# A decode step of attention plus MLP on one core: longer loops on VectorE and TensorE, side work moved to GpSimd and ScalarE, another form for the last P V

## The chip, the cores and the metric

One Trainium2 chip, of which the kernel uses one core. The metric is the device time of one execution in microseconds, the median of several runs. The profile is one more execution, recorded by the hardware profiler; its span runs from the first to the last recorded instruction, and its own device time is 1.84 us longer than that span.

## The reference

The sizes are B = 8 sequences of one token, D = 576, H = 32 heads of 128, a cache of 4096 positions, and an MLP of width 4608. All inputs are bf16.

```python
g = sigmoid((x * gate_w).sum(-1, keepdims=True))
q = (x @ wq) as [B, 32, 1, 128]
p = softmax(einsum("bhqd,bhkd->bhqk", q, k_cache) * 128 ** -0.5)
a = einsum("bhqk,bhkd->bhqd", p, v_cache) as [B, 1, 4096] @ wo
h = gelu(layernorm(x) @ w1 + b1)            # tanh form
b = h @ w2 + b2
out = g * a + (1 - g) * b
```

The two caches are 268 MB each, so nearly all of the 557 MB that the kernel reads is K and V, each byte used once.

## The kernel before, in words

**Groups.** The work is cut into 32 groups (`NG`), each of one sequence and eight heads. A group's K is 8.4 MB. It is laid out with 16 partitions per head and 256 positions per partition, and comes as two halves into the buffers KB[0] and KB[1]. Its V has the same layout and comes as one 8.4 MB transfer into VB. All large transfers stand in one hand-written order on SyncE's queue: K halves of group n+1, then V of group n+1, and so on. Each waits for the release of its buffer: a K half for the multiplication that read it last, V for the last P V matmul of the group before.

**Scores.** Eight chunks of 32 positions per group. `mult` has VectorE multiply K by the broadcast query (4096 products per partition, result in `p1`); TensorE adds up the products in eight matmuls with the identity (`held` keeps the weights in place for seven of them); `reduce` has VectorE add the last 16 partial sums. `between(c)` is the place where other work goes between the chunks: `norm` of the group before, the MLP's up projection, its down projection, and the output projection `a_proj`.

**Softmax and P V.** `softmax` finds maxima on VectorE, has ScalarE do the exponential, and has VectorE spread the weights into P with eight masked multiplications (`own`). `pv` has 64 matmuls, 32 columns of P as weights and 512 columns of V moving, into four row groups of one PSUM bank. `evict` (ScalarE) copies the bank to `O_sb`, `gather` adds the four row groups up with four fp32 matmuls, `norm` divides, `put` stores.

**The last group's V** comes in eight parts, because the end of the kernel hangs on it: half of it into KB[0], and 32, 32, 16, 16, 16, 8 and 8 positions into VB (`V_LAST`). All of its P V is in another form, `pv_turned`: one matmul per position, with V as the weights and eight columns of P moving, so that no `evict` and `gather` stand behind the last transfer.

**The MLP** shares one buffer, RB, with all weights in turn: wq, w1, w2, wo. `up_proj` (216 matmuls) stands in groups 1 to 3, `act_h` (bias and gelu, five operations on VectorE and a sigmoid on ScalarE) in group 4, `down_proj` (144 matmuls) in group 5; wo is loaded after it. `b_out` adds b2 and multiplies by 1 - g.

**The program.** A small recording layer (`Stream`) keeps one list of operations per engine and one semaphore per engine. Groups 6 to 29 (`L0`, `L1`) are emitted as a hardware loop on VectorE and TensorE (`emit_loop`), in which a wait's value grows by a fixed step with each turn; everything else is emitted in full. `head_slot` sets at which slot of a 256-slot code block the loop's first instruction stands. ScalarE, SyncE and GpSimd have no loop.

Counted in the built program, with a matmul as its weight load and its multiplication (twice that for fp32, one for a `held` one):

| instructions | TensorE | VectorE |
|---|---|---|
| ahead of the loop | about 2,185 | 241 |
| in the loop's body | 234 | 57 |
| behind the loop | about 1,075 | 71 |

## Time and profile before

| | |
|---|---|
| three runs | 1304.11, 1305.06, 1305.33 us, median 1305.06 |
| profiled execution | 1304.64 us, span 1302.8 us |
| busy: PE, DVE, ACT, POOL | 812.6, 855.5, 65.1, 1.6 us |
| mean TensorE clock granted | 0.84 |
| mean rate of HBM reads | 428 GB/s over the span |
| multiplication by q on DVE (L430), x256 | 2282 ns each |
| chunk sum on DVE (L448), x256 | 684 ns each |
| one matmul of a usual P V (L491), x1984 | 534 ns mean |

PE, PEld, DVE, ACT, POOL and SP are TensorE's multiplications, its weight loads, VectorE, ScalarE, GpSimd and SyncE. The profile has a row per DMA queue: q1 is SyncE's, q10 ScalarE's, and q8 and q14 carry the engines' own code. A share of 1.00 of the DMA engines means that all 16 are busy all the time. In a list of instructions, the first two numbers are the start and the time taken (a merged entry: of the whole run of them), and the bracket tells how long the engine was idle before and what released it. In a list of stretches, each row gives per engine the busy time and (x the number of instructions), and at its end TensorE's clock, the DMA engines' share and GB/s.

### The profile page before, as it was taken

The numbers are of one execution on the slowest core, as the hardware profiler recorded it, in microseconds if no ns is written. First come the engines' busy times: TensorE is split into PE (matmuls) and PEld (weight loads), VectorE is DVE, ScalarE is ACT, GpSimd is POOL, SyncE is SP. The second block draws the span as 40 slices with busy tenths as digits, with TensorE's granted clock in tenths as the row PEclk, the third lists the DMA queues.
The fourth block names the chain that finished last, engine by engine and source line by source line (L and its number), as shares of the span: only waits on it lengthen the run. The fifth ranks groups of instructions, "written<-read, shape, count | busy, mean of one in ns | idle before, by whom it ended". The sixth has DMA issues, their size and how long they took to land.

```text
span 1302.8 us, 10855 instructions
## 1 busy us (share of the span) xinstructions
PE 812.6 (62%) x5156; PEld 171.6 (13%) x3364; DVE 855.5 (66%) x1094; ACT 65.1 (5%) x144; POOL 1.6 (0%) x12
## 2 busy tenths in 40 slices
PE   3657776566466565665665666565666656666666
PEld 0112230111011100111110111110011110011113
DVE  4656668456666677666668666668766667766685
ACT  1100001000000000000000000000000000000000
POOL 0000000000000000000000000000000000000000
PEclk8968888678788889878888878888987898887888
DMA  9999999999999999999999999999999999999997
GB/s 401 417 451 425 440 419 427 441 431 410 442 431 431 424 433 434 443 435 433 424 433 431 440 433 435 432 428 432 433 440 429 434 428 433 434 442 429 423 432 304
DMA packets 20900, 557.25 MB, mean 428 GB/s; under 512 B 2048, under 2 KB 6160, under 8 KB 7056
## 3 DMA queue, kind: packets, MB, share of 16 engines
q1 hardware_dynamic: 20624, 556.95, 99.4%
q8 instruction: 13, 0.21, 0.1%
q10 hardware_dynamic: 256, 0.03, 0.0%
q14 instruction: 7, 0.06, 0.0%
HBM read 556.96 MB, written 0.01 MB: 428 GB/s over the span
## 4 chain that ended last, share of the span: by engine, by line
DMA 69%; DVE 18%; PE 9%; issue 3%; SPq 0%; DVEq 0%; ACT 0%
DMA KB<-in_A_k_cache_dram 67%; DVE p L430 16%; PE psb L174 7%; DVE s_sb L448 2%; DMA VB<-in_A_v_cache_dram 2%; PE psb L441 1%; SPq L257 0%; PE psb L491 0%; DVEq L132 0%; PE psb L553 0%; DVE P L477 0%; PE psb L498 0%; ACT E L474 0%; DVE mA L465 0%; PE psb L589 0%
## 5 line engine op out<-in xcount | busy, mean ns | idle before, releaser
L430 DVE TENSOR_TENSOR p<-KB,q_n 128x4096 bf16<-128x4096 bf16 x256 | 581.5, 2282 | 322.7 <-DMA KB<-in_A_k_cache_dram 313.6
L174 PE MATMUL psb<-p,ident 128*128 128x512 bf16 x1792 | 486.1, 417 | 0.0
L441 PE MATMUL psb<-p,ident 128*128 128x512 bf16 x256 | 111.1, 434 | 295.9 <-DVE p L430 295.8
L448 DVE TENSOR_REDUCE s_sb<-psb 128x32 f32<-128x512 f32 x256 | 175.2, 684 | 81.9 <-PE psb L174 81.6
L491 PE MATMUL psb<-VB,P 128*32 128x512 bf16 x1984 | 176.7, 534 | 0.0
L441 PEld LDWEIGHTS psb<-p,ident 128*128 128x128 bf16 x256 | 26.1, 102 | 718.7 <-DVE p L430 637.1
L498 PE MATMUL psb<-rs,ones 128*128 128x8 f32 x64 | 18.8, 368 | 150.9 <-DVE rs L481 150.4
L491 PEld LDWEIGHTS psb<-VB,P 128*32 128x32 bf16 x1984 | 64.3, 129 | 98.6 <-issue 83.4
L477 DVE TENSOR_SCALAR P<-E,own 128x256 bf16<-128x256 bf16 x248 | 51.4, 282 | 17.9 <-ACT E L474 17.9
L508 PE MATMUL psb<-selO,O_sb 128*128 128x8 f32 x248 | 33.6, 262 | 21.2 <-ACT O_sb L503 21.2
L498 PEld LDWEIGHTS psb<-rs,ones 128*128 128x128 f32 x64 | 15.8, 306 | 201.8 <-DVE rs L481 201.3
L418 ACT ACTIVATE q_n<-q_bc 128x128 bf16<-128x128 bf16 x32 | 9.9, 309 | 528.8 <-DVE p L430 528.8
L508 PEld LDWEIGHTS psb<-selO,O_sb 128*128 128x128 f32 x248 | 30.8, 195 | 36.1 <-ACT O_sb L503 36.1
L503 ACT ACTIVATE O_sb<-psb 128x512 f32<-128x512 f32 x31 | 18.5, 596 | 258.7 <-PE psb L491 258.7
L474 ACT ACTIVATE E<-s_sb,mD 128x256 bf16<-128x256 f32 x32 | 16.2, 507 | 143.2 <-DVE mD L473 143.2
L528 PEld LDWEIGHTS psb<-yT_sb,RB 128*128 128x128 bf16 (+1 forms) x216 | 19.4, 165 | 22.0 <-issue 20.0
L423 ACT ACTIVATE OT_sb<-O_n 128x8 bf16<-128x8 bf16 x31 | 7.4, 237 | 252.2 <-DVE O_n L514 252.2
L528 PE MATMUL psb<-yT_sb,RB 128*128 128x8 bf16 (+1 forms) x216 | 19.8, 227 | 0.0
L465 DVE TENSOR_REDUCE mA<-s_sb 128x1 f32<-128x256 f32 x32 | 13.4, 420 | 1.1
L480 DVE TENSOR_REDUCE es<-E 128x1 f32<-128x256 bf16 x32 | 13.2, 411 | 0.0
L513 DVE RECIPROCAL rz<-psb 128x8 f32<-128x8 f32 x31 | 6.2, 200 | 4.7 <-PE psb L508 4.7
L394 PE MATMUL psb<-RB,p 128*8 128x512 bf16 x40 | 5.4, 618 | 5.4 <-DMA RB<-in_A_wq_dram 5.4
(71 smaller groups left out, 100.2 us busy)
## 6 DMA issues: line engine op xcount, KB each, us to landing
KB<-in_A_k_cache_dram SPq DMA_DIRECT2D x64, 4096.0 KB, 26.8
VB<-in_A_v_cache_dram SPq DMA_DIRECT2D x2, 4096.0 KB, 23.8
RB<-in_B_w_dram SPq DMA_DIRECT2D x1, 5184.0 KB, 43.7
RB<-in_B_w_dram SPq DMA_DIRECT2D x1, 4608.0 KB, 45.5
RB<-in_A_wo_dram SPq DMA_DIRECT2D x1, 4608.0 KB, 45.4
RB<-in_A_wq_dram SPq DMA_DIRECT2D x1, 4096.0 KB, 12.6
KB<-in_A_v_cache_dram SPq DMA_DIRECT2D x1, 4096.0 KB, 17.1
VB<-in_A_v_cache_dram SPq DMA_DIRECT2D x2, 1024.0 KB, 20.3
```

The source lines that it names most:

```text
L174: return e.add_instruction(mybir.InstMatmult(name=nc.get_next_instruction_name(), engine=mybir.EngineType.PE, ins=[e.lower_ap(rhs), e.lowe ...
L430: v_mult[n, c] = op("vector", lambda e: e.tensor_tensor(out=p1[:, par, :, :], in0=KB[u % NKH][:, t0:t0 + CT, :], in1=qb, op=ALU.mult), [k_ ...
L441: fn = lambda e, r=r: e.matmul(tr_ps[par][:, :], lhsT=ident[:, :], rhs=r, start=True, stop=False)
L448: v_red[n, c] = op("vector", lambda e: e.tensor_reduce(out=s_sb[:, c * CT:(c + 1) * CT], in_=tr_ps[par][:, :].rearrange("p (t c) -> p t c" ...
L465: t = op("vector", lambda e: e.tensor_reduce(out=mA[:, 0:1], in_=s_sb[:, :], axis=AX.X, op=ALU.max), [v_red[n, NC - 1], c_mA])
L474: a_exp[n] = op("scalar", lambda e: e.activation(out=E[:, :], in_=s_sb[:, :], func=ACT.Exp, bias=mD[:, 0:1], scale=1.0), [v_nm[n], v_P.get ...
L477: v_P[n] = op("vector", lambda e, h=h: e.tensor_scalar(out=(P if n < NG - 1 else P_last)[:, :, h, :], in0=E[:, :].rearrange("p (q t) -> p ...
L491: p_pv[n] = op("tensor", lambda e, o=o, tq=tq, at=at, buf=buf: e.matmul(o, lhsT=P[:, tq, :, :].rearrange("p h t -> p (h t)"), rhs=buf[:, a ...
L498: p_z[n] = op("tensor", lambda e: e.matmul(oz_ps[:, HB:2 * HB], lhsT=ones[:, :], rhs=rs[:, :], start=True, stop=True), [v_rs[n], v_norm.ge ...
L503: a_ev[n] = op("scalar", lambda e: e.activation(out=O_sb[:].rearrange("p t d -> p (t d)"), in_=o_ps[0][:, :], func=ACT.Copy), [p_pv[n], p_ ...
L508: p_oz[n] = op("tensor", lambda e, tt=tt: e.matmul(oz_ps[:, 0:HB], lhsT=O_sb[:, tt, :], rhs=selO[:, tt, :], start=(tt == 0), stop=(tt == T ...
L528: st["p_up"] = op("tensor", lambda e, w=w, o=o, kt=kt: e.matmul(o, lhsT=w, rhs=yT_sb[:, kt, :], start=(kt == 0), stop=(kt >= NKF)), [*ld_w ...
```

## The change

1. **Loops.** VectorE's loop covers groups 1 to 29 and its first instruction stands at slot 128; TensorE's covers groups 4 to 29, at slot 16. For this each engine gets two semaphores: operations of a turn count on the first, those marked `aside` (set-up, MLP, output projection) on the second, so that a turn's counts stay regular. A first turn that lacks some waits is now allowed.
2. **Side work off VectorE.** Clearing PSUM (five banks before, three now), `Sel`, `spread` and the four copies into `g4` go to ScalarE; the gelu chain goes to GpSimd, with a copy out of PSUM by ScalarE ahead of it; `b_out` becomes a copy on ScalarE, and `b_gate`, two operations on GpSimd, takes place in group 27.
3. **The MLP earlier.** `up_proj` in groups 1 and 2, in every chunk; `act_h` and `down_proj` in group 3. w2 and wo are loaded earlier, w2 ahead of the V of group 3. b2 is loaded in group 27, as eight small transfers of five and three rows in place of four of eight rows.
4. **The last P V.** The first 192 of the 256 positions of the last group are done by `pv` with the weights `P_last` into the second bank, followed by `evict` and `gather`; the last 64 stay turned, and both parts are added up in one PSUM region (`qb_ps`). `gather` of group 30 stands ahead of it.

In the built program TensorE now has about 1,745 instructions ahead of its loop and about 800 behind it; VectorE has 53 and 72. ScalarE's list grows from 160 to 181, GpSimd's from 11 to 23, SyncE's stays at 116.

```diff
-        self.sem = {e: nc.alloc_semaphore(f"sem_{e}") for e in ("gpsimd", "scalar", "vector", "tensor")}
+        self.sem = {(e, side): nc.alloc_semaphore(f"sem_{e}{side}")
+                    for e in ("gpsimd", "scalar", "vector", "tensor") for side in range(2)}
...
-        with eng.bass.Fori(0, len(turns), engines=OrderedEngineSet([eng.engine]), head_slot={eng.engine: 0}) as k:
+        with eng.bass.Fori(0, len(turns), engines=OrderedEngineSet([eng.engine]), head_slot={eng.engine: slot}) as k:
...
+    def aside(engine, fn, waits=()):
+        return op(engine, fn, waits, side=1)
...
-    c_ps = [memset("vector", bank[i][:, :], 0.0) for i in range(4)]
-    c_yps = memset("vector", y_ps[:, :], 0.0)
+    def blank(ps):
+        return aside("scalar", lambda e: e.activation(out=ps[:, :], in_=zeros, func=ACT.Copy), [c_mA])
+
+    c_ps = [blank(tr_ps[i]) for i in range(2)]
+    c_yps = blank(y_ps)
...
+    last = NG - 1
+    UP, NUP = 1, 2
+    DN = UP + NUP
+    AP = 30
+    LOOP = {"tensor": DN + 1, "vector": 1}
+    SLOT = {"tensor": 16, "vector": 128}
...
-                o = o_ps[0][32 * j:32 * j + 32, :]
+                o = o_ps[n // last][32 * j:32 * j + 32, :]
...
-                    o, lhsT=P[:, tq, :, :].rearrange("p h t -> p (h t)"),
+                    o, lhsT=(P if n < last else P_last)[:, tq, :, :].rearrange("p h t -> p (h t)"),
...
-        t = op("vector", lambda e: e.tensor_tensor(
-            out=hb.rearrange("p (f b) -> p f b", b=B), in0=up_ps[:, 0:NJ * B].rearrange("p (f b) -> p f b", b=B),
-            in1=b1b, op=ALU.add), [st["p_up"], ld_b1])
+        t = aside("scalar", lambda e: e.activation(out=hb, in_=up_ps[:, 0:NJ * B], func=ACT.Copy), [st["p_up"]])
+        hbv = hb.rearrange("p (f b) -> p f b", b=B)
+        t = op("gpsimd", lambda e: e.tensor_tensor(out=hbv, in0=hbv, in1=b1b, op=ALU.add), [t, ld_b1])
...
-            for i in range(4)]
+            for i in range(4) for r, m in ((0, 5), (5, 3))]
...
-    UP, NUP = 1, 3
-    DN = UP + NUP + 1
-    AP = 30
-    L0, L1 = DN + 1, 30
...
     pv(last - 1, (1,))
     evict(last - 1)
-    pv_turned(last, (0,))
     gather(last - 1)
     norm(last - 1)
+    pv(last, (0,))
     total(last)
     recip(last)
-    pv_turned(last, range(1, 1 + len(V_LAST)))
+    pv(last, (1, 2))
+    evict(last)
+    pv_turned(last, (3,))
+    gather(last)
+    pv_turned(last, range(4, 1 + len(V_LAST)))
     norm_turned(last)
```

## The prediction

> **What bounds the kernel now.** I read the page's DMA rows first, then the same rows for the stretch in which both loops run, then the end of the kernel in quarters of a microsecond.

> ```profile
> span 1302.8 us, 10855 instructions
> DMA packets 20900, 557.25 MB, mean 428 GB/s; under 512 B 2048, under 2 KB 6160, under 8 KB 7056
> q1 hardware_dynamic: 20624, 556.95, 99.4%
> q8 instruction: 13, 0.21, 0.1%
> q14 instruction: 7, 0.06, 0.0%
> ...
> KB<-in_A_k_cache_dram SPq DMA_DIRECT2D x64, 4096.0 KB, 26.8
> ```

> SyncE's queue is busy 99.4% of 16 engines' span, 1295 of 1302.8 us. A K half takes 26.8 us from issue to landing, while its 4.19 MB need 9.8 us at 428 GB/s: some 17 us of earlier transfers are still ahead of it when it is issued. So between the first and the last transfer no engine's work sets the time, as long as this lead isn't used up. What remains is the DMA engines' own order, and the stretch behind the last byte.

> The code transfers are the interesting small rows. By stretch (23 to 76, 76 to 290, 290 to 1230, 1230 to 1290, 1290 to 1298 us), the rows that name code:

> ```profile
> q8 instruction: 1, 0.02, 0.1%
> q14 instruction: 1, 0.01, 0.0%
> ...
> q8 instruction: 8, 0.13, 0.2%
> q14 instruction: 3, 0.02, 0.0%
> ...
> q1 hardware_dynamic: 14446, 406.26, 100.4%
> q14 instruction: 2, 0.02, 0.0%
> ...
> q8 instruction: 2, 0.03, 0.2%
> ...
> q8 instruction: 2, 0.03, 1.7%
> ```

> q8 has nine packets before both loops run, none in 940 us of them and four behind: the pattern of TensorE's code, 2,185 instructions ahead of its loop and 1,075 behind, so one packet per 250 or so. q14's four packets up to 290 us I put down to VectorE (241 instructions and the jump into its loop), the two inside the loops to ScalarE and SyncE, which have none. One packet is short (1.7% of 16 engines in 8 us, over two packets: 1.09 us each), but it stands on one DMA engine, whose share of K and V is late from then on. A transfer is complete only when the latest engine is done. The end of the kernel shows how late:

> ```profile
> 1292.75:1293.00 0.25, 0.00 (x0) 0.00 (x0) 0.21 (x2) 0.00 (x0) 0.00 (x0) 0.50 0.80 311
> 1293.75:1294.00 0.25, 0.25 (x15) 0.25 (x14) 0.17 (x1) 0.00 (x0) 0.00 (x0) 0.50 0.56 221
> 1294.50:1294.75 0.25, 0.25 (x16) 0.25 (x14) 0.00 (x0) 0.00 (x0) 0.00 (x0) 0.50 0.33 131
> 1295.75:1296.00 0.25, 0.25 (x16) 0.25 (x14) 0.00 (x0) 0.00 (x0) 0.00 (x0) 0.50 0.07 25
> 1296.50:1296.75 0.25, 0.25 (x16) 0.25 (x14) 0.00 (x0) 0.00 (x0) 0.00 (x0) 0.50 0.02 8
> 1296.75:1297.00 0.25, 0.24 (x10) 0.15 (x6) 0.00 (x0) 0.00 (x0) 0.00 (x0) 0.50 0.00 0
> 1292.75:1297.00 4.25, 3.79 (x122) 3.70 (x122) 0.57 (x3) 0.24 (x1) 0.00 (x0) 0.50 0.34 131
> ```

> The last three numbers are TensorE's clock, the DMA engines' share and GB/s. One engine alone makes 25. The first engines finish at 1292.75; at 1294.0 about nine run, at 1294.7 five, from 1295.9 one, which ends at about 1296.8. I read steps of 1.5 us: seven engines hardly delayed, four delayed by one q8 packet, four by two, and one, 4.1 us late, by four q14 packets of about 1 us. Thirteen q8 packets over eight engines in turn give just that (the thirteenth comes when its engine is done).

> Behind the last byte:

> ```profile
> 1297.12 0.29 PEld L589 LDWEIGHTS psb<-p,VB 128*128 128x128 bf16 x8 [0.22 <-DMA VB<-in_A_v_cache_dram]
> 1297.88 1.13 PE L553 MATMUL psb<-RB,OT_sb 128*8 128x144 bf16 x32 [0.38 <-DVE OT_sb L598]
> 1299.45 0.66 SPq L257 DMA_DIRECT2D out_dram<-out_sb  x2
> ```

> TensorE waited only 0.22 us for the last eight positions: it was nearly late itself. From 1297.12 to the end at 1302.8 runs a fixed chain of 5.7 us.

> **The change part by part**, against the profiled execution's 1304.64 us.

> *Loops: minus 1.1 us.* TensorE's program shrinks to 1,745 and 800 instructions: seven packets ahead of the loop and three behind, ten for thirteen. In turn over eight engines, two engines get two and six get one. The last of the three is due some 520 instructions behind the loop, which is in the last group's P V, at about 1288 and still ahead of the last V parts. VectorE's 53 instructions end near the loop's head at slot 128, so I count one q14 packet on its engine, one or two microseconds' delay at most. The latest engine is then one with two q8 packets, which now end at about 1295.8, against 1296.8: I take 1.1 us off. Bounds: nothing, if VectorE's engine keeps four packets; and minus 2.7 us, all 16 ending together (the whole stretch from 1292.75 on moves 4.25 us at its rate in the last row, 0.56 MB, which 16 engines at 25 GB/s each move in 1.4 us, so by 1294.15). The packets that fall away free 0.06 MB, which the latest engine doesn't feel.

> [...]

> *The last P V: nothing, if it keeps pace.* These rows price it:

> ```profile
> 1283.02 1.91 PE L491 MATMUL psb<-VB,P 128*32 128x512 bf16 x32
> 1258.53 3.60 PE L491 MATMUL psb<-VB,P 128*32 128x512 bf16 x32
> 1287.58 3.40 PE L589 MATMUL psb<-p,KB 128*128 128x8 bf16 x128 [2.65 <-DVE p L477]
> 1290.84 1.85 PE L508 MATMUL psb<-selO,O_sb 128*128 128x8 f32 x8
> 1285.65 0.58 ACT L503 ACTIVATE O_sb<-psb 128x512 f32<-128x512 f32 x1
> 1228.83 4.49 DVE L430 TENSOR_TENSOR p<-KB,q_n 128x4096 bf16<-128x4096 bf16 x2 [8.73 <-DMA KB<-in_A_k_cache_dram]
> ```

> 192 turned positions at 27 ns (3.40 over 128) go, 5.1 us; 48 usual matmuls come, at 60 ns (1.91 over 32) 2.9 us, or at 113 ns (3.60 over 32, which I take for the half clock that the quarters above grant) 5.4 us, with an evict of 0.58 and a gather of 1.85. Does this end ahead of the last part? The piece that counts starts when position 192 has landed. The last 64 positions are 2.1 MB, a sixteenth of it 131 KB, 5.2 us at 25 GB/s. In these 5.2 us TensorE has to do eight P V matmuls (0.9 at half clock), ScalarE the evict (0.65 with its signal), TensorE the gather (1.85) and 40 turned ones (1.1): 4.5 us. It fits by 0.7 us, so the last eight positions still wait for their transfer. I take 0; bounds plus 0.7 us, if every wait between the engines costs 0.25 us more than in the rows, and minus 0.5, if the last projection (1.13 us at 1297.88) runs at the full clock, where the row of the same 32 matmuls below has 0.67. VectorE, which runs without a pause from the K landing at 1228.83 on, starts up to 2.5 us earlier (the latest engine is 1.6 late there, not 4.1), so P is ready before V.

> *The MLP earlier, on other engines: 0.* It lies in groups whose cover is the 17 us lead.

> ```profile
> 1269.02 0.67 PE L553 MATMUL psb<-RB,OT_sb 128*8 128x144 bf16 x32
> 96.67 1.66 PE L528 MATMUL psb<-yT_sb,RB 128*128 128x8 bf16 x18
> 97.59 0.68 DVE L448 TENSOR_REDUCE s_sb<-psb 128x32 f32<-128x512 f32 x1
> 98.19 2.28 DVE L430 TENSOR_TENSOR p<-KB,q_n 128x4096 bf16<-128x4096 bf16 x1
> 98.48 1.67 PE L174 MATMUL psb<-p,ident 128*128 128x512 bf16 x7
> 205.69 0.46 DVE L539 TENSOR_TENSOR Q<-Q 128x288 f32<-128x288 f32 x1
> ```

> A chunk costs VectorE 2.28 + 0.68, near 3 us, and TensorE 1.67 + 0.39 for the sums plus at most 1.7 for 18 up-projection matmuls, 3.8 us. Eight chunks are 30 us in place of 24, softmax and P V some 9: a group of 39 us, where its 16.8 MB take 39. K's second half is released 6 us later, of 17. w2 now stands ahead of V of group 3 on SyncE and waits for `up_proj`; V would wait for group 2's P V anyway, and w2's 5.3 MB fill the queue for 12 us meanwhile. `down_proj` waits on TensorE for w2, and the sums of chunks 6 and 7 queue behind it for about 6 us; VectorE has by then multiplied chunk 7 and so released K. On GpSimd I price five gelu operations at 0.5 us (0.46 on VectorE) up to 2 us each; ScalarE stands in its sigmoid for up to 8 us, with the next query copy and exponential queued behind it, which are due 10 us and more later. Should the lead fail, the loss would be the 6 us beyond it; I see no way to use it up.

> [...]

> *Set-up: 0.* ScalarE gets 12 operations and one more table load ahead of the query projection.

> ```profile
> 6.42 1.28 ACT L348 ACT_TABLE_LOAD   x1
> 7.72 0.20 ACT L348 ACTIVATE stat<-stat 8x1 f32<-8x1 f32 x1
> 18.64 0.60 ACT L397 ACTIVATE Q<-psb 128x512 bf16<-128x512 f32 x1 [10.72 <-PE psb L394]
> 15.14 5.37 PE L394 MATMUL psb<-RB,p 128*8 128x512 bf16 x40 [5.40 <-DMA RB<-in_A_wq_dram]
> ```

> Three table loads are 3.8 us, four operations of 0.6 and ten of 0.2 are 4.4 us: from 1.8 us on done by about 11, and the projection waits for wq until 15.1. Cover 4 us; without it the first K release would be late, again inside the lead.

> *b2 in eight transfers:* 9 KB in group 27, in the same lead; 0, bounds minus and plus 0.1.

> **Sum:** 1304.64 - 1.1 = 1303.54. The profiled execution lies 0.42 below the median of the runs, so for the median I forecast 1303.9.

> **The rivals.**
> 1. *No gain (1304.4 to 1305.5).* VectorE's jump to slot 128 needs further packets, or the P V chain at the end takes the 1.1 us up (0.7 plus half a microsecond of clock phase). For it: TensorE's wait of only 0.22 us. Against: its 4.5 of 5.2 us.
> 2. *More gain (1302.0 to 1302.5).* The doubled engines don't double, as if the packets ran over all 16: the latest is 1.5 late, 2.6 us off, 3.1 with the last projection at the full clock. For it: only ten packets. Against: the five engines left at 1294.7.
> [...]
> 4. *Slower by a used-up lead (1307 to 1310).* w2 ahead of V starves the queue in group 3 for the 3 to 6 us of the late chunks. Against: 17 us.

> **How the numbers follow.** Forecast 0.64, rivals 0.14, 0.12, 0.03 and 0.04, 0.03 for none of these. What a measurement can tell here is about 0.2%, 2.6 us: under 1302.45 faster, over 1307.67 slower. Faster has most of rival 2 (0.11) and 0.02 of the rest, 0.13. Slower has rivals 3 and 4 and 0.01 of the rest, 0.08. Within the bound lie the other 0.79. The range takes the forecast's bounds from 1302.3 (2.7 off) to 1305.7 (0.7 on), widened for the runs' own spread of 0.6 to 1301.9 and 1306.2.

> **What would show it.** Right: ten q8 packets, three of them behind 1230 us; up to two q14 packets before 60 us and none at the loops' entry; the DMA engines' rate in the last quarters falling to nothing 4.1 - 1.1, about 3 us after the first engine is done, with two engines, not five, in the last microsecond; and TensorE's last eight turned matmuls still released by the VB transfer. Wrong: q8 or q14 packets in every turn; DMA share under 0.9 anywhere between 50 and 1290 us; the last turned matmuls released by `gather`; or a last transfer that ends no earlier.

## The result, and the profile after

The changed kernel takes 1302.97 us (median of 21 runs, 1302.61 to 1304.00), the kernel before 1304.94 us (21 runs, 1304.11 to 1305.66). The ratio is 0.9986, with a 95% interval from 0.9979 to 0.9992: 1.97 us less. That lies inside the range forecast, and 0.93 us under the forecast of 1303.9. The range, 1301.9 to 1306.2, also holds the time of the unchanged kernel, so that the parts of the sum have to be looked at one by one.

First the code packets, from the page of the kernel after, in the columns packets, MB and share:

```profile
span 1301.0 us, 10743 instructions
...
q1 hardware_dynamic: 20624, 556.95, 99.6%
q8 instruction: 10, 0.16, 0.1%
...
q14 instruction: 4, 0.03, 0.0%
```

Ten q8 packets for 13, as counted, and four q14 for 7. Then the end in quarters of a microsecond (the last three numbers again TensorE's clock, the DMA engines' share, GB/s; one DMA engine alone makes 25):

```profile
1294.00:1294.25 0.25, 0.25 (x3) 0.25 (x3) 0.00 (x0) 0.00 (x0) 0.00 (x0) 0.50 0.21 82
...
1295.25:1295.50 0.25, 0.25 (x13) 0.25 (x13) 0.00 (x0) 0.00 (x0) 0.00 (x0) 0.50 0.11 41
1295.75:1296.00 0.25, 0.23 (x8) 0.23 (x8) 0.00 (x0) 0.00 (x0) 0.00 (x0) 0.50 0.04 16
1296.00:1296.25 0.25, 0.15 (x6) 0.06 (x3) 0.00 (x0) 0.00 (x0) 0.00 (x0) 0.50 0.00 0
```

At 1294.6 five engines still ran before the change; now at most two are left from 1295.25 on. The last makes 16 of an engine's 25 in the quarter from 1295.75, so it is done at about 1295.9; before, the last made 8 in the quarter from 1296.50 and was done at about 1296.6. The chain behind the last byte, in start, time taken, engine, line, operation:

```profile
1296.40 0.29 PEld L610 LDWEIGHTS psb<-p,VB 128*128 128x128 bf16 x8 [0.34 <-DMA VB<-in_A_v_cache_dram]
...
1297.07 1.13 PE L571 MATMUL psb<-RB,OT_sb 128*8 128x144 bf16 x32 [0.29 <-DVE OT_sb L619]
1298.25 0.37 DVE L699 SCALAR_TENSOR_TENSOR out_sb<-psb,g,Q 104x144 bf16<-104x144 f32 x1 [1.24 <-PE psb L571]
1298.65 0.66 SPq L262 DMA_DIRECT2D out_dram<-out_sb  x2
```

Set this against the three rows of before, and the 1.8 us by which the span shrank fall into three pieces. The last eight weight loads start 0.72 us earlier (1297.12 to 1296.40). From them to the store's issue it is 2.25 us for 2.33. And from the store's issue to the end of the span it is 1301.0 - 1298.65 = 2.35 us, where it was 1302.8 - 1299.45 = 3.35 us. This last microsecond, more than half of the gain, stands nowhere in the prediction. SyncE's waits for the store to land (total, times, longest) show it, before:

```profile
SPq L97 <- DMA out_dram<-out_sb: 2.1, 1, 2.1
```

and after:

```profile
SPq L98 <- DMA out_dram<-out_sb: 1.1, 2, 1.0
```

What the DMA engines began to move before the change, in three stretches of 0.2 us from 1300.6, 1300.8 and 1301.0 on:

```profile
DMA packets 21, 0.00 MB, mean 13 GB/s; under 512 B 21, under 2 KB 21, under 8 KB 21
...
q14 instruction: 1, 0.01, 9.6%
...
DMA packets 4, 0.00 MB, mean 3 GB/s; under 512 B 4, under 2 KB 4, under 8 KB 4
```

and after the change, from the store's issue to the end:

```profile
DMA packets 64, 0.01 MB, mean 4 GB/s; under 512 B 64, under 2 KB 64, under 8 KB 64
...
q1 hardware_dynamic: 32, 0.00, 1.2%
q10 hardware_dynamic: 32, 0.00, 1.2%
```

The store is 64 packets (two times 32). Before the change a 65th goes with them, 8 KB of code: it begins at 1300.83 and takes 0.31 us (9.6% of 16 engines in 0.2 us), 60 output packets have begun by then, and the last four begin behind it. After the change the q14 packet comes at 1298.06, ahead of the store. Whether this is the cause, and whether it is there in the usual run, is the first thing to test. (The expectations give the times of single packets 0.23 us later than these views: their 1301.06 is 1300.83 here.)

### The profile page after: what moved, and what is told of

Same layout as the page of the kernel before. It is cut to its first block, busy times and chain, and to the rows that moved or that the text cites. A ratio compares the mean times of both kernels' runs of the same rounds, so it can differ in the third digit from the quotient of the medians.

```text
span 1301.0 us, 10743 instructions
## 1 busy us (share of the span) xinstructions
PE 812.0 (62%) x5020; PEld 169.5 (13%) x3228; DVE 849.9 (65%) x1073; ACT 71.1 (5%) x160; POOL 9.6 (1%) x19
## 2 busy tenths in 40 slices
DMA packets 20894, 557.18 MB, mean 428 GB/s; under 512 B 2048, under 2 KB 6160, under 8 KB 7056
## 3 DMA queue, kind: packets, MB, share of 16 engines
q1 hardware_dynamic: 20624, 556.95, 99.6%
## 4 chain that ended last, share of the span: by engine, by line
DMA 69%; DVE 18%; PE 9%; issue 3%; SPq 0%; DVEq 0%; ACT 0%
DMA KB<-in_A_k_cache_dram 67%; DVE p L448 16%; PE psb L179 7%; DVE s_sb L466 2%; DMA VB<-in_A_v_cache_dram 2%; PE psb L459 1%; SPq L262 0%; DVEq L134 0%; PE psb L509 0%; DVE P L495 0%; PE psb L571 0%; PE psb L547 0%; PE psb L516 0%; ACT E L492 0%; DVE mA L483 0%
## 5 line engine op out<-in xcount | busy, mean ns | idle before, releaser
L448 DVE TENSOR_TENSOR p<-KB,q_n 128x4096 bf16<-128x4096 bf16 x256 | 582.0, 2284 | 318.1 <-DMA KB<-in_A_k_cache_dram 309.0
L499 DVE TENSOR_SCALAR rs<-own,es 128x8 f32<-128x8 f32 x32 | 7.5, 234 | 1.1
## 6 DMA issues: line engine op xcount, KB each, us to landing
KB<-in_A_k_cache_dram SPq DMA_DIRECT2D x64, 4096.0 KB, 26.6
VB<-in_A_v_cache_dram SPq DMA_DIRECT2D x2, 4096.0 KB, 24.8
RB<-in_A_wq_dram SPq DMA_DIRECT2D x1, 4096.0 KB, 12.6
KB<-in_A_v_cache_dram SPq DMA_DIRECT2D x1, 4096.0 KB, 18.9
```

The costliest lines, as they stand in the source:

```text
L448: v_mult[n, c] = op("vector", lambda e: e.tensor_tensor(out=p1[:, par, :, :], in0=KB[u % NKH][:, t0:t0 + CT, :], in1=qb, op=ALU.mult), [k_ ...
```

## The experiments

Differences are against runs of the kernel before on the same chip, taken together with the variant, whose medians were 1304.75, 1304.81 and 1304.78; the changed kernel's own difference is -1.97.

| kernel | median (range), us | against before | ratio (95%) |
|---|---|---|---|
| b_vslot1 | 1304.02 (1303.56 to 1304.64) | -0.73 | 0.9993 (0.9984 to 1.0002) |
| a_loop6 | 1303.53 (1303.38 to 1304.14) | -1.22 | 0.9991 (0.9982 to 1.0000) |
| a_turned | 1302.93 (1302.73 to 1303.19) | -1.82 | 0.9986 (0.9977 to 0.9995) |
| a_vslot100 | 1302.88 (1302.13 to 1303.84) | -1.87 | 0.9985 (0.9976 to 0.9994) |
| a_store | 1302.86 (1302.70 to 1304.52) | -1.95 | 0.9986 (0.9977 to 0.9995) |
| a_vjump | 1306.98 (1306.56 to 1309.89) | +2.17 | 1.0017 (1.0008 to 1.0026) |
| a_tjump8 | 1308.70 (1306.60 to 1310.52) | +3.89 | 1.0029 (1.0018 to 1.0039) |
| a_slots | 1302.75 (1302.65 to 1303.58) | -2.06 | 0.9985 (0.9976 to 0.9994) |
| b_again | 1304.87 (1304.17 to 1305.62) | +0.09 | 1.0001 (0.9992 to 1.0010) |
| a_tl10 | 1302.89 (1302.58 to 1303.64) | -1.89 | 0.9986 (0.9977 to 0.9995) |
| a_tl14 | 1304.39 (1303.94 to 1305.13) | -0.39 | 0.9999 (0.9989 to 1.0008) |
| a_best | 1302.78 (1302.24 to 1304.27) | -2.00 | 0.9985 (0.9976 to 0.9994) |

The intervals are about 1.2 us to either side, wide against differences of half a microsecond; where such a difference is read below, the profile has to carry it. b_again, the unchanged kernel, came out 0.1 us from the other runs of itself.

### The store

b_vslot1: the kernel before with one number changed.

```diff
-        with eng.bass.Fori(..., head_slot={eng.engine: 0}) as k:
+        with eng.bass.Fori(..., head_slot={eng.engine: 1 if engine == "vector" else 0}) as k:
```

> The kernel before, VectorE's loop one slot later (slot 1 for 0), nothing else. Theory S (the end of the program costs VectorE a code packet; behind slot 0 it comes at 1301.06, onto an engine that still holds output, and the store waits for it): one slot later the packet comes with VectorE's last operation, about 1299.1, ahead of the store; SyncE's wait for the store is about 1.1 us for 2.1, the last V transfer ends at 1296.8 as before, and the time is 1.0 us under the kernel before (1303.9). Rival (the packet is another engine's, or the store's 1 us has another cause, the shorter programs of ScalarE or GpSimd): the packet stays at 1301.1, SyncE waits 2.1, no change of time.

Measured: 0.73 us less than before, with an interval that still includes no difference. The waits of SyncE in its profile:

```profile
SPq L97 <- DMA out_dram<-out_sb: 1.1, 2, 1.0
```

With this one slot no code packet is left between 1296.6 us and the end, where the kernel before has one at 1300.8, and the second microsecond of the wait is gone; so the packet is VectorE's, and it is the cause of that microsecond. In this profiled execution (1304.43 us) TensorE was itself late by 0.9 us, and the reason is the clock. The stretch in which group 30's P V gives way to group 31's chunks, before:

```profile
1263.00:1265.00 2.00, 2.00 (x11) 0.10 (x1) 0.75 (x2) 0.00 (x0) 0.00 (x0) 1.00 1.12 475
```

and in b_vslot1:

```profile
1263.00:1265.00 2.00, 2.00 (x7) 0.10 (x1) 0.00 (x0) 0.00 (x0) 0.00 (x0) 0.61 1.12 475
```

The granted clock was still at half for most of these 2 us in b_vslot1 (0.61 on average) and full before, with 7 multiplications done for 11; all that follows on VectorE and TensorE is 1.0 us later.

b_again: the kernel before, unchanged, profiled a second time.

> The kernel before, unchanged, for a second profile of it. Theory S (its last code packet meets the store in the usual run): a q14 packet about 1.6 us behind the store's issue again, SyncE waits about 2.1 us for the store, last V transfer 1296.8. Rival (the meeting was a chance of the first profile): no such packet, SyncE waits 1.1, and the microsecond of the whole is elsewhere.

Measured: 1304.87 us. Its waits of SyncE:

```profile
SPq L97 <- DMA out_dram<-out_sb: 1.9, 1, 1.9
```

and its code packets between the store's issue and the end:

```profile
q14 instruction: 1, 0.01, 0.7%
```

The packet is there again, at 1300.5. Theory S holds in both profiles of before. But this profile differs from the first in another way. TensorE's weight loads of the last P V, and VectorE's operation behind them:

```profile
1293.92 3.36 PEld L589 LDWEIGHTS psb<-p,VB 128*128 128x128 bf16 x123
...
1297.40 0.19 DVE L598 TENSOR_TENSOR OT_sb<-psb,rz 128x8 bf16<-128x8 f32 x1 [3.20 <-PE psb L589]
```

123 weight loads in one run without a wait for VB: here TensorE, not the transfer, was last. The transfer itself was done by 1296.25, earlier than the 1296.6 of the first profile:

```profile
1296.25:1296.50 0.25, 0.25 (x15) 0.25 (x13) 0.00 (x0) 0.00 (x0) 0.00 (x0) 0.50 0.00 0
```

In the first profile the two ends are level.

a_store was meant to bring the meeting back in the changed kernel.

```diff
-    SLOT = {"tensor": 16, "vector": 128}
+    SLOT = {"tensor": 16, "vector": 100}
...
             S.emit_loop(name, eng, seen, SLOT[name])
+            for _ in range(27 if name == "vector" else 0):
+                eng.wait_ge(S.sem["vector", 0], 1)
```

> The changed kernel with VectorE's loop at slot 100 and 27 waits on a semaphore that is long satisfied right behind the loop, so that the program's last branch stands at slot 255, as it did before the change (a multiple of 128 ends there). Theory S (the end block's code packet meets the store): the operand chain is that of slot 100 without the waits (last turned matmuls at 1296.4, store issued at 1298.6), a q14 packet comes 1.6 us behind the store's issue, about 1300.2, SyncE waits 2.1 us for the store in place of 1.0, time 1303.9. Rival (the store's second microsecond came from something else): SyncE waits 1.0, time 1302.9.

Measured: no. VectorE fetched nothing at its end, nine of eleven executions lie at 1302.7 to 1303.0, and my rule for the slot at which a fetch falls due did not hold; what the right rule is stays open. Two executions took 1304.15 and 1304.52, and the second of these is the profiled one. Its waits of SyncE:

```profile
SPq L98 <- DMA out_dram<-out_sb: 2.9, 2, 2.8
```

and its code packets between the store's issue and the end:

```profile
q8 instruction: 1, 0.02, 1.3%
```

A packet of TensorE's code, 16 KB at 1299.4, met the store instead, and the wait is 2.8 us for 1.0. So a meeting costs time, as theory S says, but 1.8 us here instead of 1.0, and with another engine's packet. a_best below shows the same (a wait of 2.7 us, 1304.27 us in the profiled execution). Both are the slowest of their eleven executions; that such a packet also stands behind the other slow ones isn't shown.

### The loops

a_loop6: the changed kernel with both loops where they were.

```diff
-    LOOP = {"tensor": DN + 1, "vector": 1}
-    SLOT = {"tensor": 16, "vector": 128}
+    LOOP = {"tensor": 6, "vector": 6}
+    SLOT = {"tensor": 0, "vector": 0}
```

> The changed kernel with both loops from group 6 and slot 0 as before, all else changed. Theory L (code packets make the latest DMA engine): 12 or 13 q8 packets and some 4 of VectorE's q14 come back, the last V transfer ends 0.6 to 1.0 us later than with the change (1296.8 for 1296.2), the store keeps its 1.1 us, time 1303.6 to 1304.0. Rival P (the gain came from the last P V and VectorE's relief): 1303.0 as the changed kernel, the last transfer at 1296.2.

Measured: 1.22 us less than before, so the loops are worth 1.97 - 1.22 = 0.75 us (0.56 by the plain medians). Twelve q8 packets for ten, and q14 again as before the change:

```profile
q14 instruction: 7, 0.06, 0.0%
```

The quarters of its end:

```profile
1295.00:1295.25 0.25, 0.25 (x3) 0.25 (x4) 0.00 (x0) 0.00 (x0) 0.00 (x0) 0.50 0.34 131
...
1296.25:1296.50 0.25, 0.25 (x12) 0.22 (x9) 0.00 (x0) 0.00 (x0) 0.00 (x0) 0.50 0.07 25
```

and the last weight loads:

```profile
1296.99 0.29 PEld L610 LDWEIGHTS psb<-p,VB 128*128 128x128 bf16 x8 [0.35 <-DMA VB<-in_A_v_cache_dram]
```

Five engines are late again, one runs alone until 1296.5, and the last weight loads start at 1296.99 for 1296.40. SyncE's wait for the store, however, stays short (1.1 us), although VectorE's loop is back at slot 0. By the counts VectorE has 72 instructions behind its loop for 71 before the change, so that one instruction more may have done what the one slot of b_vslot1 did; that wasn't tested by itself.

That the packets go over eight engines in turn was, in the prediction, only read from the steps at the end. a_tl10 and a_tl14 put it to the test, with more straight code on TensorE and no other difference.

```diff
-    LOOP = {"tensor": DN + 1, "vector": 1}
+    LOOP = {"tensor": 10, "vector": 1}
```

(14 in a_tl14.)

> The changed kernel with TensorE's loop from group 10 for 4: six groups more in straight code, the same instructions in the same order, no jump more, 15 or 16 q8 packets for 10. Theory L (in turn over eight engines): no engine gets a third packet, so eight in place of two engines are 3 us late and the latest stays where it was; last V transfer 1296.2 to 1296.5, time 1303.0 to 1303.2. Rival (the delay goes with the number of packets, 0.19 us for each): plus 1.1, time 1304.0.

> The changed kernel with TensorE's loop from group 14: 19 q8 packets for 10. Theory L: three engines get a third packet, the latest is 4.5 us late in place of 3.0 to 3.7, last V transfer 1297.4 to 1297.7, time 1304.2 to 1304.5 (plus 1.2 to 1.5). Rival (0.19 us for each packet): plus 1.7, time 1304.6, and most of it already at 15 packets.

Measured: 1302.89 and 1304.39 us. The q8 row of a_tl10's page, and its quarters:

```profile
q8 instruction: 16, 0.26, 0.1%
```

```profile
1294.50:1294.75 0.25, 0.25 (x6) 0.25 (x6) 0.00 (x0) 0.00 (x0) 0.00 (x0) 0.50 0.53 205
1295.25:1295.50 0.25, 0.25 (x15) 0.25 (x12) 0.00 (x0) 0.00 (x0) 0.00 (x0) 0.50 0.40 156
1295.50:1295.75 0.25, 0.25 (x11) 0.20 (x8) 0.00 (x0) 0.00 (x0) 0.00 (x0) 0.50 0.08 25
```

and a_tl14:

```profile
1294.50:1294.75 0.25, 0.25 (x3) 0.25 (x2) 0.00 (x0) 0.00 (x0) 0.00 (x0) 0.50 0.56 221
1295.75:1296.00 0.25, 0.25 (x5) 0.25 (x6) 0.00 (x0) 0.00 (x0) 0.00 (x0) 0.50 0.19 74
1296.50:1296.75 0.25, 0.25 (x15) 0.25 (x13) 0.00 (x0) 0.00 (x0) 0.00 (x0) 0.50 0.19 74
1297.00:1297.25 0.25, 0.25 (x8) 0.21 (x8) 0.00 (x0) 0.00 (x0) 0.00 (x0) 0.50 0.00 0
```

Divide by 25. With 16 packets eight engines are late together (205), six at 1295.4 (156), and all are done by 1295.75: six packets more than the changed kernel, no cost. With 19 (a 20th comes behind the last byte) three engines (74) run on for another 1.3 us. The time follows the engine with the most packets, not their number: the rival of 0.19 us per packet falls with a_tl10.

This also says which loop counts. a_tl10 has more q8 packets than the kernel before (16 for 13) and is as fast as the changed kernel. So what a_loop6 lost is, by elimination, VectorE's: it has seven q14 packets, as the kernel before has (six of those come ahead of the last V transfer), the changed kernel four (three ahead of it), and a_vslot100 and a_slots below, which lose nothing, have five ahead of it. The shorter straight code of TensorE gained nothing that these runs show. No run moved VectorE's loop alone, and which engine issued each of the six isn't shown.

a_vjump does the same to VectorE, whose packets, by the theory, all fall on one engine.

```diff
+            for _ in range(3 if name == "vector" else 0):
+                with eng.bass.Fori(0, 2, ..., head_slot={eng.engine: 0}):
+                    eng.wait_ge(S.sem["vector", 0], 1)
             S.emit_loop(name, eng, seen, SLOT[name])
```

> The changed kernel with three empty loops of two turns ahead of VectorE's loop, each beginning at the next block of 256 slots: VectorE jumps three times more and does no other work. Theory L (each of VectorE's 8 KB packets makes one DMA engine about 1 us later, and a transfer ends with its latest engine): some six q14 packets more before 100 us, that engine is 7 us late instead of 1, the last V transfer ends at about 1299.8 and the time is 1306.5 (plus 3.6). Rival (what is late on one engine is made up in the 1200 us that follow, or the engines share the load): no packet early in the kernel moves its end, time 1303.0.

Measured: plus 4.0 us on the changed kernel by the medians, for six more packets (seven between 50 and 100 us in place of one). VectorE's first multiplication of group 1, in the changed kernel:

```profile
77.78 4.49 DVE L448 TENSOR_TENSOR p<-KB,q_n 128x4096 bf16<-128x4096 bf16 x2 [23.32 <-DMA KB<-in_A_k_cache_dram]
```

and in a_vjump:

```profile
81.98 4.49 DVE L448 TENSOR_TENSOR p<-KB,q_n 128x4096 bf16<-128x4096 bf16 x2 [27.36 <-DMA KB<-in_A_k_cache_dram]
```

K lands 4.2 us later at 82 us already, 0.7 us for each packet (on several engines in turn, six packets would not have added up to that), and none of it is made up in the 1200 us that follow: 0.05 MB of code, early in the kernel, cost 0.3% of its time. The profiled execution is the slowest of the eleven (1309.89 us): its last weight loads start 5.1 us later than the changed kernel's (1301.51), and SyncE waits 2.9 us for its store, where it waits 1.0 in the changed kernel; whether a code packet met this store isn't shown.

a_tjump8 was to do it with TensorE.

```diff
+        for _ in range(8 if name == "tensor" else 0):
+            with eng.bass.Fori(0, 2, ..., head_slot={eng.engine: 0}):
+                eng.wait_ge(S.sem["gpsimd", 0], 1)
         S.emit(name, eng, seen, 0, marks and marks[0])
```

> The changed kernel with eight empty loops of two turns at the head of TensorE's program, each at the next block of 256 slots: eight q8 packets more, 18 in all, in the set-up where TensorE waits for wq. Theory L (packets go over eight engines in turn, 1.5 us each): every one of the eight engines gets one more, the latest now have three, the last V transfer ends 1.5 us later at 1297.6, time 1304.4 (plus 1.5). Rival (a packet delays all engines alike or only by its bytes): eight packets are 0.13 MB, 0.3 us at the 428 GB/s of the whole, time 1303.3.

Measured: plus 5.7 us on the changed kernel by the medians, which neither theory says, because the experiment disturbed something else. TensorE's first matmul starts at 44.1 us in it and at 8.7 us in the changed kernel: the eight jumps put it off by 35.4 us, so each costs 4.4 us at least (at 8.7 us TensorE had been waiting for ScalarE), with the DMA engines' share at 1.03 from 20 to 50 us. The query projection is 31.7 us late (46.87 for 15.16), more than the 17 us of the lead, and the DMA engines run dry. Stretches of a_tjump8:

```profile
50.00:80.00 30.00, 22.44 (x99) 2.38 (x35) 22.76 (x16) 7.84 (x13) 0.00 (x0) 0.89 0.92 370
80.00:110.00 30.00, 25.01 (x203) 11.32 (x159) 23.81 (x32) 1.34 (x3) 0.00 (x0) 0.89 0.95 400
```

and of the changed kernel:

```profile
50.00:80.00 30.00, 8.14 (x74) 3.75 (x74) 5.89 (x18) 1.10 (x2) 0.00 (x0) 0.63 0.99 422
80.00:110.00 30.00, 26.73 (x172) 10.76 (x116) 24.06 (x32) 1.06 (x3) 0.00 (x0) 0.84 1.01 434
```

0.07 and 0.06 of 30 us are 3.9 us of lost transfer in these two stretches. The profiled execution is 7.0 us longer than the changed kernel's (spans of 1308.0 and 1301.0 us), and what makes up the rest wasn't taken apart. So it says nothing on the packets, but it shows what the rival "used-up lead" looks like, and that a delay of 31.7 us is enough for it.

### Where a body lies, and two candidates

a_vslot100 changes VectorE's slot to 100 (the first two lines of a_store's diff), a_slots both slots:

```diff
-    SLOT = {"tensor": 16, "vector": 128}
+    SLOT = {"tensor": 220, "vector": 64}
```

> The changed kernel with VectorE's loop at slot 100 for 128: its body now lies across slot 128, and its program ends near slot 229. If both halves stay loaded: no packet per turn, none of VectorE's near the store (the one at 1298.29 goes), time 1303.0 as the changed kernel, SyncE's wait for the store 1.0. If a back edge over a boundary of 128 fetches again: one or two 8 KB packets in each of the 29 turns, all on one DMA engine, 29 to 58 us late, time 1330 or more.

> The changed kernel with TensorE's loop at slot 220 and VectorE's at 64, where their programs stand anyway, so that neither jumps over a part of a block: nine q8 packets for ten, none of VectorE's. TensorE's loop body then lies across two blocks of 256. Theory L: one engine with two q8 packets in place of two, the last V transfer at about 1295.7 for 1296.2, time 1302.5 to 1302.7; the store as with the change. If TensorE is the bound by then: 1303.0. If a back edge over a block boundary fetches again: a q8 packet or two in each of 26 turns, over eight engines in turn, 5 to 10 us late, time 1307 to 1312.

Measured: 1302.88 and 1302.75 us. No packet per turn in either: between 290 and 1230 us a_vslot100 has one q14 packet, as the changed kernel has, and a_slots no q8 packet at all, though its TensorE body (234 instructions from slot 220 on) lies across two blocks. So these bodies could straddle two blocks without fetching again: their back edges cost no time that these runs show, where each jump to new code in a_tjump8 cost 4.4 us or more. a_slots did not save the packets that I counted (11 q8 for 9), and its last weight loads start when those of the changed kernel do.

a_best cuts the last V transfer in two and keeps slot 100:

```diff
-    V_LAST = (32, 32, 16, 16, 16, 8, 8)
+    V_LAST = (32, 32, 16, 16, 16, 8, 4, 4)
```

> The changed kernel with VectorE's loop at slot 100 (no code packet of VectorE's near the store) and the last V transfer of 8 positions cut into two of 4. The last byte comes when it did, but TensorE has 4 turned matmuls behind it in place of 8: 0.15 us less by the row of the 8 weight loads (0.29 us), at 0.05 us more for the smaller packets; time 1302.7 to 1302.9. If the smaller transfers cost more on the latest engine: 1303.1.

Measured: 1302.78 us. a_slots and a_best lie at most 0.1 us under the changed kernel by their differences to before, no more than b_again differs from other runs of the same kernel: no version here is shown to beat it.

### The last P V

a_turned: the changed kernel with the last group's P V turned throughout.

```diff
-    T_TURN = NTK + 64
+    T_TURN = 0
...
+    pv_turned(last, (0,))
     gather(last - 1)
     norm(last - 1)
-    pv(last, (0,))
     total(last)
     recip(last)
-    pv(last, (1, 2))
-    evict(last)
-    pv_turned(last, (3,))
-    gather(last)
-    pv_turned(last, range(4, 1 + len(V_LAST)))
+    pv_turned(last, range(1, 1 + len(V_LAST)))
```

> The changed kernel with the whole last P V turned as before. Theory L: TensorE still waits for the last V transfer, if by less than 0.29 us; time 1303.0, at most 0.3 more. Rival P (the usual form is what makes TensorE keep pace with an earlier last transfer): TensorE comes late by 0.5 to 1.0 us, the last eight turned matmuls no longer wait for VB, time 1303.5 to 1304.

Measured: 1302.93 us, the changed kernel's time. Its last weight loads:

```profile
1296.35 0.29 PEld L610 LDWEIGHTS psb<-p,VB 128*128 128x128 bf16 x8 [0.34 <-DMA VB<-in_A_v_cache_dram]
```

They still wait for the transfer, and as long as in the changed kernel (0.34). With the loops in place the new form of P V gains nothing.

## Why the prediction was right, and where it was not

**Loops, minus 1.1.** The mechanism was right: ten q8 packets, three behind the loop (the first of them at 1227 us), one q14 at 58 us, two engines left in the last microsecond, and by a_tl10 and a_tl14 the eight engines in turn. The prediction had the latest engine of before late by VectorE's packets and not by TensorE's, and a_tl10 bears that out; but "four q14 packets of about 1 us" was mis-sized, at 0.7 us a packet (a_vjump) four make 2.8 us and the six ahead of the last V transfer 4.2, if all six share the engine, where 3.8 to 4.1 were to be explained. The size of the gain was off as well. The step was "which now end at about 1295.8, against 1296.8": the new end is 1295.9 and the old one was 1296.6, since a row of 8 GB/s in a quarter is an engine that stops in its first third; in b_again it was no later than 1296.25. So the last weight loads came 0.72 us earlier, and undoing the loops costs 0.56 to 0.75 us, inside the bounds of nothing to 2.7.

**"A fixed chain of 5.7 us".** This step failed. The chain from the last weight loads to the end is 4.6 us after the change (1301.0 - 1296.40), because VectorE's last code packet fell into the output store before and does not after: one slot of its loop moves it out (b_vslot1), and by the wait of 1.1 us it is out in a_loop6 too, with the loops where they were. I had put a price on every packet ahead of the last byte and looked at none behind it, though the page counted seven q14 packets and I named six. It is 1.0 us between the two profiles, and 0.73 us in the medians (b_vslot1).

**The last P V, nothing.** Right on top of the loops (a_turned). But the reading beneath it, that TensorE waits 0.22 us for the transfer and so the transfer decides, holds for one profiled execution of the kernel before and not for the other (b_again): there TensorE comes last. By the differences to before, what b_vslot1 and the loops leave is 1.97 - 0.73 - 0.75, about 0.5 us, the distance between b_vslot1 and a_loop6. It fits a TensorE that is no longer late, but how much of it belongs to the form of P V and how much to the K that lands earlier wasn't taken apart, and it is small against the intervals. VectorE's multiplication behind that K landing:

```profile
1226.51 4.49 DVE L448 TENSOR_TENSOR p<-KB,q_n 128x4096 bf16<-128x4096 bf16 x2 [9.39 <-DMA KB<-in_A_k_cache_dram]
```

It starts 2.3 us earlier than before (1228.83); the prediction had up to 2.5. With that cover TensorE keeps pace in either form, which fits a_turned, where the old form costs nothing.

**MLP, set-up, b2: nothing.** The query projection starts at 15.16 us for 15.14, and from 50 to 110 us and on to 1230 us the DMA share stays at 0.99 and above. GpSimd's slowest and quickest gelu operations:

```profile
L558 POOL TENSOR_SCALAR Q<-Q 128x288 f32<-128x288 f32 x1 | 2.3, 2345 | 0.1
...
L557 POOL TENSOR_TENSOR Q<-Q 128x288 f32<-128x288 f32 x1 | 0.7, 665 | 0.1
```

Two of the five were above the 2 us that I took as the bound (2.35 and 2.25), a guess of mine that no row of before gave; the other three are at 0.7 to 0.8. They are 6.7 us together, and the lead covers it.

**The rivals.** "No gain" and "more gain" are out by the quarters and by a_tl10: the latest engine is 0.7 us better, and the packets run over eight engines, not 16 (205 GB/s at 25 each with 16 packets). The third rival (chance 0.03) was a loop that fetches code in each turn; no run shows one. Between 290 and 1230 us the changed kernel has one q8 and one q14 packet in all, and a_slots no q8 and two q14, with a TensorE body across two blocks. "Used-up lead" did not happen; in a_tjump8 a delay of 32 us did it.

So the forecast came out 0.93 us high: the loops gave 0.4 less than written, the store and a TensorE that is no longer late gave more than 1 that was not written at all. That two misses of opposite sign left the time near the forecast is luck.

## What to carry to other kernels

Where transfers keep all DMA engines busy, read the packets of code as well: here each sat on one engine, and a transfer ended with the latest (in a_tl14 three engines ran on for 1.3 us, and the last weight loads came 1.3 us later than in a_tl10). What counted was how many fell on the same engine, not how many there were (16 packets in a_tl10 took no longer than ten), and whether one fell into the output store, where one slot was worth as much as the longer loops (0.73 us in b_vslot1, 0.75 by a_loop6). A second profile of the kernel before is cheap when two chains end within a quarter of a microsecond of each other: which of them decided changed here from one execution to the next.
